# Identity products on the tensor engine in the waits of a kernel's first ten slots

## The chip, the cores and the metric

The kernel runs on one core of a Trainium2 chip. The metric is the device time of one execution in microseconds. A core has a tensor engine (PE, with its weight loads shown apart as PEld), a vector engine (DVE), a scalar engine (ACT), a general engine (POOL) and a queue engine for transfers (SP). Each takes its instructions in the order in which the program issues them, and waits for the results of others by semaphores. The profile also shows the clock that PE was granted, as a share of its full speed.

## What is computed

Top-k attention over 8 batches, 8 heads, 576 positions and 64 elements per head, and behind it an MLP with an exact GELU on 4608 tokens (512 to 2048 to 512). All is f32.

```python
scores = scale * np.matmul(q, k.transpose(0, 1, 3, 2))
kth = np.partition(scores, -32, axis=-1)[..., -32:-31]
scores = np.where(scores >= kth, scores, -1e9)
attn = softmax(scores)                      # over the last axis
x = (attn @ v).transpose(0, 2, 1, 3).reshape(4608, 512)
h = x @ w_in
out = (0.5 * h * (1 + erf(h / sqrt(2)))) @ w_out
```

## The kernel before

**Items and slots.** Heads are taken in pairs. An item is one tile of 128 query rows for the two heads of a pair (or the 64-row tails of two pairs together): 144 items. The main loop (line 651) runs over slots n, and each slot works on several items at different stages: scores of item n+2, softmax of item n-1, transposes of item n-2, attention of item n-3, top-k of item n. Order is written out by hand: the pool is scheduled manually, so each engine's instructions stand in the order of the code.

**A slot on PE**, in order: `scores` (a 128x128 product t_ps, line 283, and products s_ps, line 287); `attend` (o, line 466; only where an item completes a pair of row tiles: slots 4, 6, 8 and 10 among the first eleven; the variable `product` tells it); then `transposes` in three pieces, first the tail (tp_t, line 411), then one main piece of four transposes per head (tp, line 429); and, where due, pieces of `transpose_qk` for later pairs (tp_qk, line 242), which `prep` holds. In between `mlp(1)` issues pieces of the MLP (h_ps, line 518; y_ps, line 554), as far as finished tokens allow. The first 256 tokens are finished by the attention of slot 10 (START is 10), so in slots 0 to 9 these calls issue nothing.

**A slot on ACT**: copies of the scores out of PSUM (lines 297 and 298), softmax of the first head (lines 379 and 380), the copy of an attention product into xT (line 471), softmax of the second head, copies of the tail and the main transposes (lines 412 and 436), copies of q/k pieces (line 246), and up to slot 16 the conversion of a unit of weights (`weights_size`, lines 175 to 179).

**DVE** does the top-k: eight MAX8 (line 340) and six MATCH_REPLACE8 (line 343) per item, and at its end the reciprocal of the denominator of the item before (line 366). **POOL** adds the weight words (lines 194 and 206), adds a small number to the denominators (line 372), computes the threshold and the bias (lines 355 and 358) and multiplies the item before by the reciprocals (`normalise`, line 392); the tail transpose of that item needs this product.

**PSUM.** t_ps, o, tp_t, tp and tp_qk share two buffers of the tag tp, so each waits until the one before last has been copied away. s_ps has one buffer. h_ps has two of the tag l1, unused until slot 10 except by the warming products below.

**Before the loop** line 630 issues nine (WARM) products of a zero tile, then the q/k pieces of two pairs and the scores of items 0 and 1.

Of the kernel before, what the change touches and what calls it, by code (L numbers as in the profile page):

```python
# [14 lines left out]
def kernel(  # L15
# [19 lines left out]
    nc = tc.nc  # L35
    f32, i32, u32 = mybir.dt.float32, mybir.dt.int32, mybir.dt.uint32
# [5 lines left out]
    P = 128  # L42
# [19 lines left out]
    ps = ctx.enter_context(tc.tile_pool(name="ps", bufs=2, space=bass.MemoryType.PSUM))  # L62
    ctx.enter_context(tc.manual_schedule())

    ident = const.tile([P, P], f32, name="ident")
# [59 lines left out]
    START = 2 * NP + 2  # L125
    WARM = 9
# [54 lines left out]
    def on_pool(u):  # L181

        return u in words and SLOT_OF[u] >= START + 2
# [3 lines left out]
    def weights_add(u):  # L187
        if u in words:
            w, _, below, d = parts(u)
            if on_pool(u):  # L190
                nc.gpsimd.tensor_scalar(
                    w.bitcast(i32), w.bitcast(u32), 2.0**-13, None, op0=ALU.mult
                )
            nc.gpsimd.tensor_tensor(d, d, below, op=ALU.add)
            if not ends_late(u):
                weights_end(u)
        made.add(u)

    def ends_late(u):

        return u in words and SLOT_OF[u] <= START

    def weights_end(u):
        if u in words:
            w, _, _, d = parts(u)
            nc.gpsimd.tensor_tensor(d, d, w.bitcast(i32), op=ALU.add)
# [118 lines left out]
    def top_k(i, hooks):  # L325


        stat_of[i] = st = {
            "top": work.tile([P, 2, TOPK], f32, tag="top", name="top"),
            "neg": work.tile([P, 2, 2], f32, tag="neg", name="neg"),  # L330
            "bias": work.tile([P, 2], f32, tag="bias", name="bias"),
            "den": work.tile([P, 2], f32, tag="den", name="den"),
            "rden": work.tile([P, 2], f32, tag="rden", name="rden"),
        }
        cur = [row(i, e) for e in range(2)]
        rest = work.tile([P, 2, S], f32, tag="rest", bufs=1, name="rest")
        n_op = 0
        for r in range(TOPK // 8):
            for e in range(2):
                nc.vector.max(st["top"][:, e, 8 * r : 8 * r + 8], cur[e])  # L340
            if r < TOPK // 8 - 1:
                for e in range(2):
                    nc.vector.match_replace(  # L343
                        rest[:, e], st["top"][:, e, 8 * r : 8 * r + 8], cur[e], LOWEST
                    )
                cur = [rest[:, e] for e in range(2)]
            if r in hooks:
                hooks.pop(r)()

    def threshold(i):  # L350

        if i < 0 or i >= N:
            return
        st = stat_of[i]
        nc.gpsimd.tensor_scalar(  # L355
            st["neg"], st["top"][:, :, 0 :: TOPK - 1], -1.0, None, op0=ALU.mult
        )
        nc.gpsimd.tensor_tensor(
            st["bias"], st["neg"][:, :, 0], st["neg"][:, :, 1], op=ALU.subtract
        )  # L360

    def inverse(i):
        if i < 0 or i >= N:
            return
        st = stat_of[i]
        nc.vector.reciprocal(st["rden"], st["den"])  # L366

    def add_small(i):
        if i < 0 or i >= N:
            return  # L370
        st = stat_of[i]
        nc.gpsimd.tensor_scalar(st["den"], st["den"], 1e-9, None, op0=ALU.add)  # L372

    def softmax(i, e):

        if i < 0 or i >= N:
            return
        st, s = stat_of[i], row(i, e)
        nc.scalar.activation(s, s, func=AF.Prelu, bias=st["neg"][:, e, 1:2], scale=1.0, alpha=STEEP)  # L379
        nc.scalar.activation(  # L380
            s, s, func=AF.Exp, bias=st["bias"][:, e : e + 1], scale=1.0,
            accum_out=st["den"][:, e : e + 1],
        )
# [16 lines left out]
    def transposes(i):  # L400

        if i < 0 or i >= N:
            return []
        t, s = items[i][1], S_of.pop(i)

        def tails():
            tp = ps.tile([P, 512], f32, tag="tp", name="tp_t")
            if t < NM:
                if t % 2 == 0:
                    pt_now[0] = work.tile([P, 2 * NM + 1, 2 * P], f32, tag="pt", name="pt")  # L410
                nc.tensor.transpose(tp[:, 0:P], s[:, SM : S + TL], ident)  # L411
                nc.scalar.copy(out=pt_now[0][:, 2 * NM, t % 2 * P : (t % 2 + 1) * P], in_=tp[:, 0:P])  # L412
            else:
                pt_now[0] = ptt
                for r in range(2):
                    nc.tensor.transpose(
                        tp[0:TL, r * P : (r + 1) * P], s[:, r * S + SM : (r + 1) * S], ident
                    )
                for e in range(2):
                    c = slice(e * TL, (e + 1) * TL)  # L420
                    nc.scalar.copy(
                        out=halves(ptt[c, 0, NM, :], e, NJ * P), in_=halves(tp[0:TL, 0 : 2 * P], e, P)
                    )

        def main(e):
            tp = ps.tile([P, 512], f32, tag="tp", name="tp")
            first = e * (S + TL if t < NM else S)
            for j in range(NM):
                nc.tensor.transpose(  # L429
                    tp[:, j * P : (j + 1) * P], s[:, first + j * P : first + (j + 1) * P], ident  # L430
                )
            if t < NM:
                dst = pt_now[0][:, e * NM : (e + 1) * NM, t % 2 * P : (t % 2 + 1) * P]
            else:
                dst = ptt[:, e, 0:NM, :]
            nc.scalar.copy(out=dst, in_=tp.rearrange("p (j n) -> p j n", j=NM))  # L436

        return [tails] + [lambda e=e: main(e) for e in range(2)]

    def copy_x():  # L440
        while copies:
            copies.pop()()
# [149 lines left out]
    def run_gelus():  # L592
        while waiting:
            gelus(waiting.pop(0))
# [9 lines left out]
    def mlp(n):  # L604
        for _ in range(n):
            if done[0] >= len(pieces) or pieces[done[0]][0] > ready[0] or left[0] == 0:
                return
            pieces[done[0]][1]()
            done[0] += 1
            left[0] -= 1  # L610
            if eager[0]:
                run_gelus()
# [12 lines left out]


    idle = raws["v"][0][:, NM].rearrange("p e d -> p (e d)")
    warm = ps.tile([P, 512], f32, tag="l1", name="warm")
    for _ in range(WARM):
        nc.tensor.matmul(warm[:, 0:P], lhsT=idle, rhs=idle, start=True, stop=True)  # L630
    for pair in range(2):
        for piece in transpose_qk(pair, pair == 0):
            piece()
# [17 lines left out]
    for n in range(ahead):  # L651

        left[0] = 4 if n in (START, START + 1) else 8
        eager[0] = n > N
        weights_add(unit_in(n))
        scores(n + 2)
        product = attend(n - 3)
        late = n > START
        if n <= START:

            softmax(n - 1, 0)
        copy_x()
        mlp(1)
        tr = transposes(n - 2)
        if product and n > START and done[0] < len(pieces) and pieces[done[0]][0] > ready[0]:

            for piece in tr[:1]:
                piece()
            tr, ready[0] = tr[1:], n_tok[0]
        if n > START:  # L670
            softmax(n - 1, 0)
        mlp(1)
        if not late:
            softmax(n - 1, 1)
        mlp(1)
        prep = prep_in.pop(n, [])
        if len(prep) > 1 and len(tr) == 3:
            tr, prep = tr[:1] + prep[:1] + tr[1:], prep[1:]
        for piece in tr[:-1]:
            piece()  # L680
            ready[0] = n_tok[0]
            mlp(1)
        ready[0] = n_tok[0]
        if late:
            softmax(n - 1, 1)
        add_small(n - 1)
        if ends_late(unit_in(n)):
            weights_end(unit_in(n))
        for piece in tr[-1:] + prep:
            piece()  # L690
            mlp(1)

        run_gelus()
        mlp(left[0])
        run_gelus()
        if n < N:
            top_k(n, {3: lambda: inverse(n - 1)})
        else:
            inverse(n - 1)
        threshold(n)  # L700
        u = unit_in(n + 1)

        normalise(n - 1, 2 if on_pool(u) else 0)

        weights_size(unit_in(n + 1))
        if n >= FIRST:
            load_weights(n + 2)
        if n <= NP:
            load("v", n)
# [38 lines left out]
```

## Time and profile before

| quantity | value |
|---|---|
| median of 5 runs | 1642.16 us (1640.52 to 1642.37) |
| the profiled execution | 1640.55 us, span 1638.8 us |
| PE busy | 1587.8 us (97% of the span) |
| DVE busy | 1415.3 us (86%) |
| ACT busy | 1186.2 us (72%) |
| POOL busy | 662.3 us (40%) |
| mean granted PE clock | 0.979 |

The span is from the first to the last instruction on the engines. In the lines of the profile, L12 is line 12 of the kernel; out<-in are the program's names; a bracket shows how long the engine stood idle before the instruction and what ended that.

### The profile page before, as it was taken

The numbers are of one execution on the slowest core, as the hardware profiler recorded it, in microseconds if no ns is written. First come the engines' busy times: TensorE is split into PE (matmuls) and PEld (weight loads), VectorE is DVE, ScalarE is ACT, GpSimd is POOL, SyncE is SP. The second block draws the span as 40 slices with busy tenths as digits, with TensorE's granted clock in tenths as the row PEclk, the third lists the DMA queues.
The fourth block names the chain that finished last, engine by engine and source line by source line (L and its number), as shares of the span: only waits on it lengthen the run. The fifth ranks groups of instructions, "written<-read, shape, count | busy, mean of one in ns | idle before, by whom it ended". The sixth has DMA issues, their size and how long they took to land.

```text
span 1638.8 us, 25030 instructions
## 1 busy us (share of the span) xinstructions
PE 1587.8 (97%) x8818; PEld 1075.5 (66%) x8818; DVE 1415.3 (86%) x3046; ACT 1186.2 (72%) x2133; POOL 662.3 (40%) x759
## 2 busy tenths in 40 slices
PE   6679999999999999999999999999999999999999
PEld 4346676766666666676666667676666666666665
DVE  8999999988898889998989898998889889999800
ACT  6999877777777777777777777777777777777720
POOL 4897633333333333333333333333333333333300
PEclk7779999999999999999999999999999999999999
DMA  6433210011101120001100111001110101000000
GB/s 164 141 112 122 55 43 1 14 32 41 35 1 28 30 50 8 14 16 36 30 28 15 28 30 43 1 14 32 41 36 1 28 16 35 1 14 3 6 13 13
DMA packets 126765, 56.14 MB, mean 34 GB/s; under 512 B 117776, under 2 KB 118064, under 8 KB 126640
## 3 DMA queue, kind: packets, MB, share of 16 engines
q1 hardware_dynamic: 125376, 54.12, 12.3%
q8 instruction: 70, 1.15, 0.3%
q14 instruction: 55, 0.45, 0.1%
q10 hardware_dynamic: 1200, 0.39, 0.1%
q0 software_dynamic: 64, 0.03, 0.0%
HBM read 45.08 MB, written 9.44 MB: 33 GB/s over the span
## 4 chain that ended last, share of the span: by engine, by line
PE 91%; ACT 5%; POOL 1%; issue 1%; DVE 1%; DMA 1%; SPq 0%; ACTq 0%; POOLq 0%; DVEq 0%
PE y_ps L554 30%; PE h_ps L518 30%; PE o L466 9%; PE tp L429 8%; PE s_ps L287 8%; PE tp_qk L242 2%; PE t_ps L283 2%; PE o L477 1%; ACT s L380 1%; PE s_ps L314 1%; PE tp_t L411 1%; ACT s L379 1%; POOL s L392 1%; ACT w_in_sb L175 1%; ACT s L297 1%
## 5 line engine op out<-in xcount | busy, mean ns | idle before, releaser
L340 DVE MAX8 top<-rest 128x8 f32<-128x576 f32 x864 | 609.6, 747 | 0.0
L518 PE MATMUL h_ps<-xT,w_in_sb 128*128 128x256 f32 (+1 forms) x2560 | 553.0, 361 | 0.0
L554 PE MATMUL y_ps<-w_out_sb,g 128*128 128x512 f32 x1152 | 548.9, 599 | 0.0
L392 POOL TENSOR_SCALAR s<-s,rden 128x576 f32<-128x576 f32 x278 | 476.4, 1723 | 0.6 <-DVE rden L366 0.4
L518 PEld LDWEIGHTS h_ps<-xT,w_in_sb 128*128 128x128 f32 x2560 | 428.4, 191 | 61.8 <-issue 16.8
L343 DVE MATCH_REPLACE8 rest<-top,rest 128x576 f32<-128x576 f32 x576 | 423.5, 743 | 0.0
L372 POOL TENSOR_SCALAR den<-den 128x2 f32<-128x2 f32 x144 | 32.0, 222 | 836.7 <-ACT s L380 836.3
L554 PEld LDWEIGHTS y_ps<-w_out_sb,g 128*128 128x128 f32 x1152 | 195.1, 190 | 168.2 <-issue 167.3
L297 ACT ACTIVATE s<-s_ps 128x1024 f32<-128x1024 f32 x127 | 130.5, 1028 | 164.3 <-PE s_ps L287 142.1
L380 ACT ACTIVATE s<-s,bias 128x576 f32<-128x576 f32 x288 | 223.6, 776 | 13.2 <-ACT s L379 0.7
L379 ACT ACTIVATE s<-s,neg 128x576 f32<-128x576 f32 x288 | 224.5, 779 | 0.3 <-POOL neg L355 0.2
L436 ACT COPY pt<-tp 128x512 f32<-128x512 f32 x256 | 147.5, 576 | 101.5 <-PE tp L429 101.5
L429 PEld LDWEIGHTS tp<-ident,s 128*128 128x128 f32 x1152 | 145.6, 144 | 101.0 <-issue 58.9
L343 DVE MATCH_REPLACE8 rest<-top,s 128x576 f32<-128x576 f32 x288 | 211.8, 743 | 0.0
L340 DVE MAX8 top<-s 128x8 f32<-128x576 f32 x288 | 201.8, 742 | 1.4 <-ACT s L293 1.4
L429 PE MATMUL tp<-ident,s 128*128 128x128 f32 x1152 | 178.0, 278 | 14.2 <-ACT pt L412 11.6
L466 PE MATMUL o<-pt,raw_v 128*64 128x256 f32 x1280 | 155.7, 390 | 0.0
L287 PE MATMUL s_ps<-qk 64*128 64x256 f32 x1024 | 152.5, 418 | 0.8 <-ACT s L295 0.8
L366 DVE RECIPROCAL rden<-den 128x2 f32<-128x2 f32 x144 | 23.1, 161 | 138.3 <-POOL den L372 138.0
L466 PEld LDWEIGHTS o<-pt,raw_v 128*64 128x64 f32 x1280 | 87.8, 139 | 66.5 <-issue 22.6
L287 PEld LDWEIGHTS s_ps<-qk 64*128 64x128 f32 x1024 | 91.9, 194 | 23.7 <-issue 1.6
L529 ACT ACTIVATE g<-h_ps 128x512 f32<-128x512 f32 x144 | 78.6, 595 | 37.8 <-PE h_ps L518 37.1
(71 smaller groups left out, 1075.2 us busy)
## 6 DMA issues: line engine op xcount, KB each, us to landing
raw_q<-in_q_dram SPq DMA_DIRECT2D x64, 128.0 KB, 2.4
raw_v<-in_v_dram SPq DMA_DIRECT2D x64, 128.0 KB, 2.4
w_out_sb<-in_moe_w_in_dram SPq DMA_DIRECT2D x16, 511.8 KB, 4.9
raw_k<-in_k_dram SPq DMA_DIRECT2D x62, 128.0 KB, 2.4
out_dram<-y SPq DMA_DIRECT2D x31, 256.0 KB, 2.2
w_out_sb<-in_moe_w_out_dram SPq DMA_DIRECT2D x10, 511.8 KB, 3.9
words<-in_moe_w_out_dram SPq DMA_DIRECT2D x6, 511.8 KB, 4.5
out_dram<-y SPq DMA_DIRECT2D x9, 128.0 KB, 2.3
```

Of the source, the lines that this page charges most:

```text
L287: nc.tensor.matmul(s_ps[:, e, c * 256 : (c + 1) * 256], lhsT=lhsT[rows, :], rhs=qk[rows, KT + c * 256 : KT + (c + 1) * 256], start=True, s ...
L297: nc.scalar.activation(spread(s, S + TL, SM), s_ps, func=AF.Copy, scale=scale)
L340: nc.vector.max(st["top"][:, e, 8 * r : 8 * r + 8], cur[e])
L343: nc.vector.match_replace(rest[:, e], st["top"][:, e, 8 * r : 8 * r + 8], cur[e], LOWEST)
L379: nc.scalar.activation(s, s, func=AF.Prelu, bias=st["neg"][:, e, 1:2], scale=1.0, alpha=STEEP)
L380: nc.scalar.activation(s, s, func=AF.Exp, bias=st["bias"][:, e : e + 1], scale=1.0, accum_out=st["den"][:, e : e + 1],)
L392: (nc.vector if e >= 2 - on_dve else nc.gpsimd).tensor_scalar(s, s, st["rden"][:, e : e + 1], None, op0=ALU.mult)
L429: nc.tensor.transpose(tp[:, j * P : (j + 1) * P], s[:, first + j * P : first + (j + 1) * P], ident)
L436: nc.scalar.copy(out=dst, in_=tp.rearrange("p (j n) -> p j n", j=NM))
L466: nc.tensor.matmul(o[e * D : (e + 1) * D, 0:n], lhsT=vt[:, j, e, :], rhs=pt[:, e * NM + j if j < NM else 2 * NM, :], start=(j == 0), stop= ...
L518: nc.tensor.matmul(h_tile(u)[:, i, :], lhsT=w_in_sb[:, ko, f * P : (f + 1) * P], rhs=xT[:, ko, c0 : c0 + n], start=(ko == 0), stop=(ko == ...
L554: nc.tensor.matmul(y_of[sub], lhsT=g_of[u][:, i, sub * P : (sub + 1) * P], rhs=w_out_sb[:, f, :], start=(f == 0), stop=(f == FT - 1),)
```

## The change

A helper `keep_busy` issues a number of products of one matrix with itself into a PSUM tile that nobody reads; the warming products before the loop now go through it. In slots 0 to 9 the loop calls it with the identity: 8 products in slot 0 and in slots with an attention product, 28 in the others, ahead of the transposes; 10 more behind the tail transpose in slots with an attention product; and 24 at the end of slot 1's pieces.

```diff
     idle = raws["v"][0][:, NM].rearrange("p e d -> p (e d)")
-    warm = ps.tile([P, 512], f32, tag="l1", name="warm")
-    for _ in range(WARM):
-        nc.tensor.matmul(warm[:, 0:P], lhsT=idle, rhs=idle, start=True, stop=True)
+
+    def keep_busy(count, m):
+        warm = ps.tile([P, 512], f32, tag="l1", name="warm")
+        for _ in range(count):
+            nc.tensor.matmul(warm[:, 0:P], lhsT=m, rhs=m, start=True, stop=True)
+
+    keep_busy(WARM, idle)
...
         mlp(1)
+        if n < START:
+
+            keep_busy(8 if product or n == 0 else 28, ident)
         prep = prep_in.pop(n, [])
...
         for piece in tr[:-1]:
             piece()
+            if n < START and product and piece is tr[0]:
+                keep_busy(10, ident)
             ready[0] = n_tok[0]
             mlp(1)
...
         for piece in tr[-1:] + prep:
             piece()
             mlp(1)
+        if n == 1:
+            keep_busy(24, ident)
```

## The prediction

> **What bounds the kernel now.** First the page's slices (41 us each; digits are tenths busy): they part the run into two regimes.
>
> ```profile
> PE   6679999999999999999999999999999999999999
> DVE  8999999988898889998989898998889889999800
> ACT  6999877777777777777777777777777777777720
> PEclk7779999999999999999999999999999999999999
> ```
>
> From the fourth slice on PE is full at the full clock; only the first three slices (the ten slots that the change touches) have PE slack and a granted clock near 0.7. So no gain or loss arises late, but any shift of the moment at which PE fills up is carried to the end one for one.
>
> Next the busy time in the stretches between the steps of the clock (columns: stretch, length, busy time and count of each engine, granted clock, DMA share, GB/s).
>
> ```profile
> 17.64:55.10 37.46, 22.66 (x88) 14.90 (x90) 37.46 (x81) 32.62 (x52) 27.68 (x24) 0.50 0.50 128
> 55.10:65.30 10.20, 4.40 (x33) 2.62 (x29) 10.02 (x23) 9.62 (x17) 8.04 (x8) 1.00 0.71 231
> 65.30:72.10 6.80, 5.41 (x23) 3.78 (x25) 6.80 (x15) 6.02 (x11) 6.44 (x6) 0.51 0.31 71
> 72.10:79.00 6.90, 4.20 (x33) 2.51 (x31) 6.90 (x16) 6.52 (x13) 5.84 (x5) 0.99 0.37 137
> 79.00:92.60 13.60, 8.50 (x37) 5.38 (x37) 13.60 (x31) 12.69 (x19) 13.00 (x12) 0.50 0.37 120
> 103.00:113.20 10.20, 7.66 (x31) 5.00 (x33) 10.20 (x23) 9.32 (x18) 9.33 (x9) 0.50 0.29 86
> ```
>
> The clock is either whole or half, and stretches are multiples of about 3.4 us. DVE is full throughout: a slot of top-k is 9.7 us on DVE whatever PE does. ACT is nearly as full. A warm PE can therefore win only where ACT or PE, not DVE, decides.
>
> Third the order of time on ACT and PE around slots 2 and 3.
>
> ```profile
> 29.20 0.80 PE L283 MATMUL t_ps<-qk 128*128 128x128 f32 x2 [2.82 <-ACT qk L246]
> 29.93 2.08 PE L287 MATMUL s_ps<-qk 64*128 64x256 f32 x8
> 35.16 0.48 PE L411 MATMUL tp_t<-ident,s 128*128 128x128 f32 x1 [3.16 <-DMA w_out_sb<-in_moe_w_in_dram]
> ```
> ```profile
> 32.49 1.00 ACT L297 ACTIVATE s<-s_ps 128x1024 f32<-128x1024 f32 x1
> 36.75 0.25 ACT L412 COPY pt<-tp_t 128x128 f32<-128x128 f32 x1
> 48.97 0.59 ACT L436 COPY pt<-tp 128x512 f32<-128x512 f32 x1 [0.72 <-PE tp L429]
> ```
>
> Scores 4 leave PE at 32.01, and ACT, working without a break, takes them at 32.49: 0.5 us in hand. The DMA named on the third line had long landed; POOL's normalisation of item 0 ended at 35.1, and that is what PE waited for. ACT's only waits in the slots are the bracketed ones on PE's transposes: 0.72 us at half clock, 0.26 us in warm slots.
>
> Last, in the chain of waits, the price of 128-column f32 passes in a long row.
>
> ```profile
> 291.21 2.68 PE h_ps L518 x24
> 293.89 0.22 PE t_ps L283 x2
> ```
>
> **The change part by part.** The sum is made against the profiled execution, 1640.55 us (span 1638.8 and 1.75 around it). The median, 1642.16, is 1.6 above it; the runs lie in two clusters, 1640.5 and 1642.2.
>
> *Price of a product.* An f32 product of 128 columns is two passes. 24 passes in 2.68 us are 0.112 each, so 0.223 a product at the full clock (t_ps: 0.22). The far ends: the nine products of line 630 stood 3.67 us, 0.41 each; a transpose (one pass) steps on in 0.11. I take 0.223, the row with the same shape and the longest run. Blocks: 8 are 1.8 us, 10 are 2.2, 24 are 5.4, 28 are 6.25. In all 8+52+28+28+3x18+3x28 = 254 products, 57 us, beside PE's 43.7 us of idle time in the first 110 us (110 less 66.3 busy); they fit only if old work runs warm.
>
> *Slot 0.* Eight products run from 16.5 to 18.3, inside the 2.42 us wait for raw_k (next start 18.97): hidden. The clock, which fell at 17.64 in the trace, should hold; then tp_qk takes 0.65 instead of 1.09, and ACT, which waits for it, starts its conversion 0.44 earlier.
>
> *Slot 1.* PE: tp_qk 0.44, t_ps 0.22, s_ps 1.06 from 18.97 reach 20.7. 28 products end at 26.95; the two q/k pieces (0.22 and 0.44) at 27.6, their ACT copies due at 27.9 (28.31 less 0.44): still hidden. Then 24 more to 33.0. Behind them in PE's order stand scores 4: 0.22 + 1.14 to 34.3. ACT is ready at 32.05 and now waits 2.3 us; everything behind on ACT (softmax 1, copies, weight conversions) stands with it. L297 comes at 34.4 instead of 32.49: **+1.9**.
>
> *Slot 2.* 28 products from 34.25 to 40.5, but POOL is done near 35, so these delay the tail transpose of item 0 from 35.16 to 40.5, done 40.75. ACT would be there at 38.65: 2.1 us more, **+4.05** in all. Warm transposes give 0.45 back: **+3.6**.
>
> *Slots 3 to 9.* Without an attention product PE needs, from ACT's tail copy on: main transposes 0.44, scores 0.22 + 1.06, 28 products 6.25, tail 0.11, first main 0.66: 8.75 us; with one: 0.44 + 1.28 + 2.31 + 1.8 + 0.11 + 2.2 + 0.66 = 8.8. A slot is 9.7, so both stay about 0.9 us inside it and cost nothing; that cover goes if the clock halves, and then 28 products are about 12 us. Gain: the 0.72 us waits of slots 3, 5, 7 and 9 become 0.26: 4 x 0.46, to **+1.75**. POOL's add to the denominator waits for ACT, so DVE's reciprocal, which stood with 0.18 us to spare in slot 4, makes DVE wait about 3 us in slots 3 and 4. That is covered: DVE later idles 1.53, 1.00, 1.00 and 2.00 us (128, 140, 163, 185) and gives them up first. No DMA is moved; the loads are issued by the same steps, and SP's queue has nothing new. The new tiles use the l1 buffers, idle until slot 10.
>
> *Slot 10.* It has an attention product and no filler. Attention ends near 114.0; the tail needs POOL's item 8 (113.1 plus 2.4: 115.5), the first MLP product ACT's xT copy (114.66 plus 1.75 plus 0.36: 116.8). PE stands idle for nearly 3 us, just where before it was dense at half clock and then warm. The nearest row is the fall at 17.64, 1.1 us into an idle stretch and after a thin one; so I take a fall, and of the shortest stretch, 3.4 us, half is lost on work that the chain passes through (114.8 to 118.8 are MLP products and transposes on the chain): **+1.7**. Ends: 0, and 3.4 for two stretches.
>
> [...]
>
> *Sum.* 1.75 + 1.7 = 3.45 above 1640.55: **1644.0 us**. From 138 on PE is without a gap until 182, and again from 204, so the shift stays.
>
> **The rivals.**
>
> *Faster: the blocks are hidden in slots 1 and 2.* Place: PE ahead of scores 4 and of tail 0. It turns on the price of one product: ACT loses nothing if 80 products, 2.2 us of other work (0.66 q/k, 1.28 scores, 0.27 tail) from 20.7 on end by 36.3, a price of about 0.167 us. For it: transposes step in 0.11, and these products use one stationary operand over and over. Against: 24 passes of the same shape cost 0.112 each. Then only the gains stay: 0.44 + 5 x 0.46 = 2.7, 1637.9 us, and up to 3.3 with the warm scores of slot 10: 1637.2. Chance 0.24.
>
> *Clearly slower: the clock falls early or twice.* If it is half from 17.6 to 24.5 as in the trace, the first block costs up to 2.8 us more: 1646.8; two stretches at slot 10 instead give 1645.7, a stretch lost in slots 3 to 9 about 1.2 more. For it: a window with 55% PE busy (1.88 of 3.4 us, 75.7 to 79.1) was followed by half clock. Against: filled slots have PE over 85% busy. Chance 0.31.
>
> *The products don't keep the clock, or cost 0.41 throughout.* 28 products are then about 12 us, beyond the slot: several us in each of seven slots, some 45 us in all, 1690. Against: after line 630's products the transposes at 5.28 ran four in 0.63, the warm duration. Chance 0.03.
>
> The forecast keeps 0.42, its own range 1642.3 to 1645.4.
>
> **How the numbers follow.** A measurement of this kernel tells 0.2% (3.3 us) from nothing: 1638.9 to 1645.4 is "within". The forecast lies within it whole (0.42); of the faster rival 0.20 lies below 1638.9 and 0.04 within; of the clearly slower one 0.29 lies above and 0.02 within; the last is above. So faster 0.20, within 0.48, slower 0.32. The range reaches from the faster rival's 1637.5 to 1648, an early fall together with one at slot 10; about 0.2 is left out.
>
> **What would show it.** Clock 1.00 from 14.6 to 113; products at 0.22; ACT's L297 at 34.4 with a wait on s_ps of 2.3, its L412 near 40.8 with a wait on the tail of 2.1; the 0.72 us waits gone; a DVE wait on the denominator in slots 3 or 4; a cold stretch after 114. Wrong if ACT runs through slots 1 and 2 without waiting, if a product's price isn't 0.22, or if the clock steps elsewhere.

## The result, and the profile after

The changed kernel takes 1643.86 us (median of 30 executions, 1643.57 to 1645.57); the kernel before, run beside it, 1640.89 us (median of 50, 1639.76 to 1642.57). The ratio is 1.0020, with a 95% interval of 1.0015 to 1.0025: slower by some 3 us. The interval leaves out 1, so a loss is there, but the time lies inside what the prediction called "within" (1638.9 to 1645.4). Before's times spread from 1639.8 to 1642.6, with 14 of the 50 under 1640.2 and 13 over 1642.0; of the five runs behind the 1642.16 shown earlier, three lay over 1642.0. The profiled execution of after took 1643.92 us, against 1640.55 us of the one before: +3.37 us.

The page's slices of after, 41 us each, first:

```profile
PE   8999999999999999999999999999999999999999
DVE  7999999988898989998989888998889888999800
ACT  5999877777777777777777777777777777777620
PEclk9999999999999999999999999999999999999999
```

The change did what it says: PE is full and its granted clock whole from the first slices on, where before they showed 6, 6, 7 and a clock of 7. The busy time by stretch confirms it (columns as before: stretch, length, busy time and count of PE, PEld, DVE, ACT and POOL, granted clock, DMA share, GB/s):

```profile
17.64:55.10 37.46, 36.27 (x303) 33.14 (x304) 35.05 (x77) 30.20 (x48) 23.73 (x22) 1.00 0.45 118
55.10:113.20 58.10, 56.63 (x466) 47.72 (x462) 57.30 (x124) 55.42 (x91) 52.55 (x41) 1.00 0.40 128
113.20:130.00 16.80, 14.25 (x90) 10.74 (x88) 16.80 (x38) 15.57 (x26) 15.70 (x12) 1.00 0.45 128
```

In the first stretch PE went from 22.66 us busy at half clock to 36.27 at the whole one. Yet ACT did less in the same 37.46 us, 30.20 instead of 32.62, POOL too (23.73 for 27.68), and DVE was no longer full (35.05). The work came later, on a faster PE. The order of time says where; PE first (L632 is the line of the products; x56 are 28 of them, two passes each):

```profile
20.86 6.52 PE L632 MATMUL warm<-ident 128*128 128x128 f32 x56
27.87 5.52 PE L632 MATMUL warm<-ident 128*128 128x128 f32 x48
33.23 0.39 PE L283 MATMUL t_ps<-qk 128*128 128x128 f32 x2
33.55 1.14 PE L287 MATMUL s_ps<-qk 64*128 64x256 f32 x8
34.61 6.52 PE L632 MATMUL warm<-ident 128*128 128x128 f32 x56
40.97 0.27 PE L411 MATMUL tp_t<-ident,s 128*128 128x128 f32 x1
```

From 20.86 to 40.97 PE works without a pause, and most of it is products that nobody reads. The scores of item 4 stand behind 52 of them, the tail transpose of item 0 behind 28 more. ACT pays (the bracket is its idle time and what ended it):

```profile
34.73 1.02 ACT L297 ACTIVATE s<-s_ps 128x1024 f32<-128x1024 f32 x1 [2.39 <-PE s_ps L287]
41.27 0.27 ACT L412 COPY pt<-tp_t 128x128 f32<-128x128 f32 x1 [2.16 <-PE tp_t L411]
43.79 1.27 ACT L175 ACTIVATE w_in_sb<-w_out_sb,low 128x1024 int32<-128x1024 int16 x1
```

Before, neither copy waited, and they started at 32.49 and 36.75. DVE, which was full before, now waits too:

```profile
52.01 0.17 DVE L366 RECIPROCAL rden<-den 128x2 f32<-128x2 f32 x1 [2.41 <-POOL den L372]
62.61 0.17 DVE L366 RECIPROCAL rden<-den 128x2 f32<-128x2 f32 x1 [0.80 <-POOL den L372]
```

The chain of waits between 17 and 45 us (start, length, what) is made of these products:

```profile
20.93 6.45 PE warm L632 x56
...
28.03 5.36 PE warm L632 x48
...
33.62 1.06 PE s_ps L287 x8
34.68 6.45 PE warm L632 x56
41.13 0.11 PE tp_t L411
```

A conversion of weights on ACT (line 175) starts once a slot and is a good clock hand for the shift. The start of that conversion, from the orders of time of several kernels:

| kernel | slot 1 | 2 | 3 | 4 | 5 | 6 | 7 | 8 | 9 | 10 | 11 |
|---|---|---|---|---|---|---|---|---|---|---|---|
| before | 20.57 | 29.04 | 39.83 | 50.30 | 59.95 | 69.57 | 79.05 | 88.67 | 98.61 | 108.52 | 119.27 |
| after | 20.16 | 28.71 | 43.79 | 54.08 | 63.85 | 73.17 | 82.70 | 91.93 | 102.27 | 111.78 | 122.63 |
| after less before | -0.41 | -0.33 | +3.96 | +3.78 | +3.90 | +3.60 | +3.65 | +3.26 | +3.66 | +3.26 | +3.36 |
| without the 24 (e1_no24) | 20.02 | 28.56 | 39.38 | 49.67 | 60.35 | 69.57 | 79.13 | 88.36 | 98.71 | 108.20 | 119.04 |
| e6_best | 20.04 | 28.58 | 38.74 | 48.89 | 58.66 | 67.98 | 77.56 | 86.80 | 97.31 | 106.81 | 117.67 |

The whole loss arises between slots 2 and 3; slots 3 to 10 give 0.60 us of it back; +3.36 at slot 11 is what the end shows too (+3.37).

### The profile page after: what moved, and what is told of

It is laid out like the page before. It is cut to its first block, busy times and chain, and to the rows that moved or that the text cites. A ratio compares the mean times of both kernels' runs of the same rounds, so it can differ in the third digit from the quotient of the medians.

```text
span 1642.2 us, 26046 instructions
## 1 busy us (share of the span) xinstructions
PE 1625.9 (99%) x9326; PEld 1121.5 (68%) x9326; DVE 1415.4 (86%) x3046; ACT 1187.8 (72%) x2133; POOL 662.6 (40%) x759
## 4 chain that ended last, share of the span: by engine, by line
PE 93%; ACT 3%; POOL 1%; DVE 1%; issue 1%; SPq 0%; DMA 0%; ACTq 0%; DVEq 0%; POOLq 0%
PE y_ps L554 30%; PE h_ps L518 30%; PE o L466 8%; PE s_ps L287 8%; PE tp L429 7%; PE warm L632 2%; PE tp_qk L242 2%; PE t_ps L283 2%; PE o L477 1%; PE tp_t L411 1%; PE s_ps L314 1%; ACT s L380 1%; POOL s L392 1%; ACT s L379 1%; ACT w_out_sb L179 0%
## 5 line engine op out<-in xcount | busy, mean ns | idle before, releaser
L297 ACT ACTIVATE s<-s_ps 128x1024 f32<-128x1024 f32 x127 | 130.6, 1028 | 166.7 <-PE s_ps L287 144.5
L429 PE MATMUL tp<-ident,s 128*128 128x128 f32 x1152 | 173.0, 273 | 2.4 <-ACT pt L412 1.8
L466 PE MATMUL o<-pt,raw_v 128*64 128x256 f32 x1280 | 152.3, 384 | 0.0
L287 PE MATMUL s_ps<-qk 64*128 64x256 f32 x1024 | 145.2, 402 | 0.8 <-ACT s L295 0.8
L529 ACT ACTIVATE g<-h_ps 128x512 f32<-128x512 f32 x144 | 78.6, 595 | 37.8 <-PE h_ps L518 37.1
L287 PEld LDWEIGHTS s_ps<-qk 64*128 64x128 f32 x1024 | 88.1, 186 | 22.0 <-ACT s L295 1.0
```

What stands on the lines that cost most here:

```text
L287: nc.tensor.matmul(s_ps[:, e, c * 256 : (c + 1) * 256], lhsT=lhsT[rows, :], rhs=qk[rows, KT + c * 256 : KT + (c + 1) * 256], start=True, s ...
L297: nc.scalar.activation(spread(s, S + TL, SM), s_ps, func=AF.Copy, scale=scale)
L429: nc.tensor.transpose(tp[:, j * P : (j + 1) * P], s[:, first + j * P : first + (j + 1) * P], ident)
L466: nc.tensor.matmul(o[e * D : (e + 1) * D, 0:n], lhsT=vt[:, j, e, :], rhs=pt[:, e * NM + j if j < NM else 2 * NM, :], start=(j == 0), stop= ...
```

## The experiments

The theory: the products are worth little as warmers, because DVE and ACT, not PE, set a slot; they cost where the program's order on PE puts them ahead of something that ACT waits for, and that is in slots 1 and 2. The rivals: the time was lost in slots 3 to 9 (conversions slowed, the denominators late); it was lost to the clock at slot 10; or the products' own kind matters. Where a kernel has fewer or other products, only work that nobody reads is left out. Times stand beside the kernel before, run on the same chip, whose median was 1640.9 beside e1 to e4 and 1641.2 beside the others.

**The block of 24, alone taken away.**

```diff
-        if n == 1:
-            keep_busy(24, ident)
```

> The block of 24 products at the end of slot 1 is left out; the rest is as in the changed kernel. Theory (scores 4 stand behind the block on PE, and ACT stands behind scores 4): the wait of 2.39 us on ACT at L297 goes, and the wait of 2.16 us at L412 in slot 2 shrinks to about 0.4, since the 28 products of slot 2 then run from 30.1 to 36.4 and ACT wants the tail at 36.3. That is 4.2 to 4.4 us back: about 1639.5, 1.4 us below the kernel before. Rival A (the cost is spread: the products lengthen ACT's instructions and waits in every filled slot): only the 2.4 us come back, about 1641.5. Rival B (the block is needed to keep the clock): half clock after 31, a block of 28 takes 12 us somewhere, over 1645.

Measured: 1640.6 us, ratio 0.9999 (0.9990 to 1.0008): all of the loss is gone with 24 of 254 products. ACT's order of time:

```profile
32.03 1.03 ACT L297 ACTIVATE s<-s_ps 128x1024 f32<-128x1024 f32 x1
36.86 0.27 ACT L412 COPY pt<-tp_t 128x128 f32<-128x128 f32 x1 [0.45 <-PE tp_t L411]
60.35 1.25 ACT L175 ACTIVATE w_out_sb<-w_out_sb,low 128x1024 int32<-128x1024 int16 x1 [0.79 <-DMA w_out_sb<-in_moe_w_out_dram]
```

The wait before L297 is gone, the one before L412 fell from 2.16 to 0.45 us, and slot 3 begins 4.41 us earlier than in after (39.38 for 43.79). At slot 6 only 3.60 of that is left: the third line shows why. ACT, now early, waits 0.79 us for a transfer of weights that SP issued at 54.80. The 3.60 and this wait together are the 4.4 us, and the wait is about the 0.8 us by which the profiled run (1640.32) lies over the expected 1639.5.

**Fewer products where one wait was left.** Besides the 24, slot 2 has 20 instead of 28.

```diff
-            keep_busy(8 if product or n == 0 else 28, ident)
+            keep_busy(8 if product or n == 0 else 20 if n == 2 else 28, ident)
...
-        if n == 1:
-            keep_busy(24, ident)
```

> The block of 24 is left out and slot 2 has 20 products in place of 28, which end at 34.6, before POOL has normalised item 0. Theory: both waits of ACT in slots 1 and 2 are gone, 0.4 us less than without the 24 alone: about 1639.0, 1.9 us below the kernel before; ACT reaches L175 of slot 3 about 0.9 us earlier than before (39.83). Rival A (spread cost): no lower than 1641.5. Rival C (DVE's slots decide the first 120 us, so a warm clock gains nothing): 1640.9, the time before.

Measured: 1641.62 us, 1639.25 to 1643.17, ratio 1.0003 (0.9994 to 1.0012). Slot 3 starts at 38.65, 0.73 us ahead of e1, where 0.4 was expected; but ACT waits for the weights again (0.58 us), and the times fall apart by their mean granted clock: 1639.3 to 1639.5 in the two runs at 1.000, 1639.8 and 1640.1 at 0.999, 1641.6 to 1643.2 in the seven at 0.998 and under. The profiled one has a fall, right behind slot 11. Busy time by stretch:

```profile
123.47:126.88 3.41, 1.41 (x11) 0.86 (x9) 3.14 (x7) 3.38 (x9) 3.24 (x3) 1.00 0.84 258
126.88:130.29 3.41, 3.34 (x14) 2.10 (x16) 3.07 (x7) 3.38 (x6) 2.93 (x4) 0.50 0.89 362
```

A stretch of 3.41 us in which PE was busy for 1.41 is followed by 3.41 us at half clock. The longest pause in it was this one, 1.39 us, the idle time before t_ps:

```profile
126.95 0.80 PE L283 MATMUL t_ps<-qk 128*128 128x128 f32 x2 [1.39 <-ACT pt L436]
```

So the gain from slot 2 is real, and the runs at the whole clock come near the expected 1639.0. That new falls at the first slots behind the products take it away in most runs is read off the mean clocks; only the profiled run shows where its fall lies.

**Products in slots 0 to 2 alone.**

```diff
-        if n < START:
+        if n < 3:
...
-            if n < START and product and piece is tr[0]:
+            if n < 3 and product and piece is tr[0]:
```

> Products only in slots 0, 1 and 2 (8, 28 and 24, 28); none in slots 3 to 9. Theory: ACT is 4.0 us late at L175 of slot 3 as in the changed kernel, and the later slots, cold again as in the kernel before, give nothing back: 1640.9 + 4.0 = 1644.9, about 1 us above the changed kernel. Rival A (the cost lies in every filled slot): faster than the changed kernel, 1642 to 1643. ACT's conversions (L175 to L179) in slots 3 to 9 should show whether the 0.02 to 0.04 us that they are longer in the changed kernel come from the products.

Measured: 1647.08 us (1646.03 to 1648.05), ratio 1.0039 (1.0026 to 1.0051), 2.2 us more than expected. In the profiled run (1648.05 us) a part of that has nothing to do with the edit: the clock fell already in slot 0 (granted 0.80 from 14.20 to 17.55 and 0.70 from there to 21.00), where e3 and after have the same products (the 16 passes there took 3.04 us instead of 2.05) and slot 3 began at 45.16, 1.37 us later than in after. From there to slot 11 it took 80.98 us; after took 78.84 and before 79.44. Two groups of lines on ACT over these eight slots, e3 first (columns: busy us, mean ns of one | idle time before), then after:

```profile
L177 ACT ACTIVATE w_out_sb<-w_out_sb,high 128x1024 int32<-128x1024 int16 x8 | 9.9, 1236 | 0.3
L436 ACT COPY pt<-tp 128x512 f32<-128x512 f32 x16 | 9.4, 585 | 4.3 <-PE tp L429 4.3
```
```profile
L177 ACT ACTIVATE w_out_sb<-w_out_sb,high 128x1024 int32<-128x1024 int16 x8 | 10.3, 1283 | 0.3
L436 ACT COPY pt<-tp 128x512 f32<-128x512 f32 x16 | 9.2, 587 | 1.9 <-PE tp L429 1.6
```

Without the products ACT waits 2.7 us longer for main transposes (4.3 for 1.6), and its conversions are shorter, 1236 ns as before. So the products of slots 3 to 9 are worth 80.98 - 78.84 = 2.1 us against no products (0.97 of it a wait for weights that e3 has and after has not), and 0.6 us against the kernel before. That rival falls: slots 3 to 9 are a gain, though a small one.

**The block of 24 doubled.**

```diff
-            keep_busy(24, ident)
+            keep_busy(48, ident)
```

> The block at the end of slot 1 is doubled, from 24 to 48 products. Theory: the block is on the chain product by product, so 24 more at 0.227 us cost 5.4 us: 1643.9 + 5.4 = 1649.3, ACT's wait at L297 grows from 2.4 to 7.8 us, and DVE's wait for the denominator in slot 3 from 2.4 to about 8. Rival D (there is slack on DVE, which idles 5.5 us later, that takes up the delay): well under 1649, about 1646.

Measured: 1651.41 us (1649.6 to 1651.89), ratio 1.0065 (1.0051 to 1.0079). ACT's order of time:

```profile
39.85 1.02 ACT L297 ACTIVATE s<-s_ps 128x1024 f32<-128x1024 f32 x1 [7.75 <-PE s_ps L287]
46.40 0.27 ACT L412 COPY pt<-tp_t 128x128 f32<-128x128 f32 x1 [2.17 <-PE tp_t L411]
```

The wait grew from 2.39 to 7.75 us: by 5.36, which is 24 times 0.223. The lowest run, which is the profiled one, is 5.8 us over after's usual 1643.8; 0.54 of that is a wait for weights in slot 5. The median is 7.5 us over after's; the three slowest runs have mean clocks of 0.998 and 0.999, and what they lost was not traced. With no slack of ACT left, each of the 24 products cost its own length, 0.223 us, and nothing downstream gave it back.

**Products into slots 10 and 11.** Six ahead of the tail transpose of slot 10, six at the end of slot 11, in another PSUM tile.

```diff
+        if n == START:
+            keep_busy(6, ident, "l2")
...
+        if n == START + 1:
+            keep_busy(6, ident, "l2")
```

> The changed kernel with 6 products more in slot 10, ahead of the tail transpose (a wait of 1.34 us), and 6 at the end of slot 11 (a wait of 1.39 us). Theory (a third of the changed kernel's runs, 1645.2 us at a mean clock of 0.999, lose the clock for one stretch of 3.4 us in the thin slots 10 and 11): the upper group goes, all runs lie at 1643.8 with a clock of 1.000. Rival E (the clock falls somewhere in slots 0 to 9): two groups as before. Rival F (any product in slots 10 and 11 delays the MLP's products behind it): 1 to 2 us above 1643.8.

Measured: 1643.94 us (1643.74 to 1644.74), ratio 1.0016 (1.0007 to 1.0025). Nine of 11 runs lie at 1643.7 to 1644.2 with a mean clock of 1.000, two at 1644.7 with 0.999. After has 20 of 30 at 1643.6 to 1644.0 and ten at 1644.9 to 1645.6, again with 0.998 or 0.999. So filling the slots behind the products doesn't lower the usual time: that time holds no loss to the clock. That it thins out the upper group is possible, but two of 11 and ten of 30 don't tell it.

**The products as transposes.** Each identity product becomes two transposes of the identity (in this kernel the products' line is 636).

```diff
-            nc.tensor.matmul(warm[:, 0:P], lhsT=m, rhs=m, start=True, stop=True)
+            if m is idle:
+                nc.tensor.matmul(warm[:, 0:P], lhsT=m, rhs=m, start=True, stop=True)
+            else:
+                for h in range(2):
+                    nc.tensor.transpose(warm[:, h * P : (h + 1) * P], m, ident)
```

> The changed kernel with each product of the identity (two passes) replaced by two transposes of it (one pass each, the same 0.22 us); the nine products before the loop stay. If the clock follows how full PE is, whatever it does: 1643.9 and a clock of 1.000. If transposes do not count as work for the clock, as the long cold stretch from 17.6 to 55.1 in the kernel before suggests (38.1 to 41.5 was 97% busy, half of it transposes, and stayed cold): the clock falls near 17 and blocks of 28 take 12.5 us at half clock, more than a slot: some 45 us more in all, about 1690.

Measured: 1643.53 us (1642.96 to 1645.76), ratio 1.0018 (1.0009 to 1.0028). PE's order of time and two stretches of it:

```profile
20.62 6.33 PE L636 MATMUL warm<-ident 128*128 128x128 f32 x56
27.44 5.40 PE L636 MATMUL warm<-ident 128*128 128x128 f32 x48
```
```profile
100.00:110.00 10.00, 9.74 (x82) 8.66 (x81) 10.00 (x22) 9.44 (x16) 8.90 (x8) 1.00 0.28 105
130.00:140.00 10.00, 9.35 (x51) 6.69 (x52) 9.05 (x21) 9.85 (x16) 8.46 (x7) 0.83 0.30 122
```

Two transposes cost nearly what one product does (28 pairs took 26.79 - 20.62 = 6.17 us, 28 products 6.35), and they hold the clock through slot 9 as well (1.00 from 100 to 110). The fall comes behind them, after 130 (0.83 from 130 to 140). For the clock the kind of filler made no difference here (the run's mean clock is 0.999).

**Products from slot 3 on only.** None in slots 0 to 2, the block of 24 gone with them.

```diff
-        if n < START:
+        if 3 <= n < START:
...
-        if n == 1:
-            keep_busy(24, ident)
```

> Products only from slot 3 on (no block in slots 0, 1 and 2, nor the 24). Theory: slots 1 and 2 run as in the kernel before, without ACT's waits, but slot 3's block of 28 starts at half clock near 42.5; with two stretches of 3.4 us until the clock rises it ends near 52.5 in place of 49, and ACT, due at the tail at 47.5, waits 5 us: 1640.9 + 5 - 0.6 = 1645. Rival A (the cost lies in every filled slot, not in slots 1 and 2): 1643 to 1644, with no wait of ACT over 1 us in slot 3. Rival H (the cold start costs nothing): 1640.

Measured: 1642.79 us (1640.87 to 1646.31), ratio 1.0014 (1.0005 to 1.0023), with mean clocks of 0.989 to 0.994. Slot 3's block starts at half clock (granted 0.50 from 30.00 to 43.30, 1.00 from there to 50.00):

```profile
42.57 6.84 PE L632 MATMUL warm<-ident 128*128 128x128 f32 x56
```
```profile
49.56 0.27 ACT L412 COPY pt<-tp_t 128x128 f32<-128x128 f32 x1 [1.78 <-PE tp_t L411]
```

In the profiled run it rose 0.7 us into the block, so 28 products took 6.84 us and ACT waited 1.78 us, not the 5 expected of a block that runs cold for longer. The runs over 1645.9 have the lowest clocks (0.989). This block came out the longer for starting at half clock (after's 28 in slot 2 took 6.52 us), just when it was not yet of use.

**The version put together.** No block of 24, 22 products in slot 2, six each in slots 10 and 11, and in slot 3 SP issues the next unit of weights ahead of the q and k loads (line numbers of the helper and below are shifted by nine).

```diff
+    put_off, slot = [], [-1]
+    def loads_now():
+        while put_off:
+            x = put_off.pop(0)
+            load("q", x)
+            load("k", x)
...
-                load("q", pair + 2)
-                load("k", pair + 2)
+                put_off.append(pair + 2)
+                if slot[0] != 3:
+                    loads_now()
...
-            keep_busy(8 if product or n == 0 else 28, ident)
+            keep_busy(8 if product or n == 0 else 22 if n == 2 else 28, ident)
+        if n == START:
+            keep_busy(6, ident, "l2")
...
-        if n == 1:
-            keep_busy(24, ident)
+        if n == START + 1:
+            keep_busy(6, ident, "l2")
...
             load_weights(n + 2)
+        loads_now()
```

> No block of 24, 22 products in slot 2 in place of 28, the products in slots 10 and 11 as in the run before, and in slot 3 the weight load is issued ahead of the q and k loads in SP's queue. Theory: ACT waits in slots 1 and 2 gone (-4.4 from 1643.8), clock held in every run, and the wait of 0.6 to 0.8 us for the weights at slot 5 gone: 1638.8, 2.1 us below the kernel before (1640.9), with a spread under 1 us. Rival C (a warm clock gains nothing, DVE decides): 1640 or more. Rival G (with ACT earlier, POOL's normalisation or another load becomes the next wait): 1639.5.

Measured: 1639.02 us (1638.71 to 1643.08), against 1641.23 beside it, ratio 0.9991 (0.9982 to 0.9999): 0.3% under after, and under before by 2.2 us of medians, which is less than the 0.2% that one measurement tells; the interval only just leaves out 1. Six of 11 runs lie at 1638.7 to 1639.0, below the lowest of 33 runs of before (1639.88). SP's order of time, e6 first, then before, shows the weights 5 us earlier:

```profile
49.43 0.82 SPq L160 DMA_DIRECT2D w_out_sb<-in_moe_w_out_dram  x2
```
```profile
54.43 0.98 SPq L160 DMA_DIRECT2D w_out_sb<-in_moe_w_out_dram  x2
```

ACT takes them without a wait at 58.66, 1.29 us ahead of before. The run at 1643.08 has a mean clock of 0.995: falls still come now and then, and the expected spread of under 1 us was missed. The move of the loads was not tried by itself.

## Why the prediction was right, step by step

The sum was 1644.0 us; the profiled run gave 1643.92, the median 1643.86. The case that came true is the forecast: the blocks of slots 1 and 2 delay ACT. But two terms of the sum were off, in opposite directions.

- *The price of a product* (0.223 us). 28 of them with the start of the next piece took 27.21 - 20.86 = 6.35 us, 0.227 each; 24 took 33.23 - 27.87 = 5.36, 0.223 each. Right. It refutes the faster rival, whose blocks fit below 0.167, and the one with 0.41.
- *Slot 0* (hidden, 0.44 earlier). The clock held, and ACT's first conversion started at 20.16 instead of 20.57: 0.41 earlier. Right.
- *Slot 1* (a wait of 2.3, L297 at 34.4, +1.9). Wait 2.39, L297 at 34.73, +2.24. Right in kind, 0.33 low: the first block started 0.16 later (20.86 for 20.7) and took 0.1 more, and the scores behind the 24 took 0.1 more.
- *Slot 2* (a wait of 2.1, L412 at 40.8, +4.05, then 0.45 back to +3.6). Wait 2.16, L412 at 41.27, +4.52, slot 3 at +3.96: right in kind, 0.36 low, of which 0.33 came from slot 1. e1 and e4 show that the two waits are nearly all that the block of 24 does: without it the waits shrink by 2.39 and 1.71 us and slot 3 starts 4.41 us earlier, and 24 more add 5.36 to the first wait.
- *Slots 3 to 9* (four waits of 0.72 become 0.26; 1.84 back, to +1.75). This term failed in size: 0.60 came back. The waits did shrink as predicted; ACT's waits for PE over these slots, before first, then after (total us, times, longest):

```profile
ACT pt L436 <- PE tp L429: 3.9, 8, 0.7
ACT qk L246 <- PE tp_qk L242: 1.0, 2, 0.7
```
```profile
ACT pt L436 <- PE tp L429: 1.6, 6, 0.5
ACT qk L246 <- PE tp_qk L242: 1.1, 3, 0.7
ACT pt L412 <- PE tp_t L411: 0.2, 1, 0.2
```

  That is 4.9 to 2.9 us, 2.0 less. But ACT's busy time over the same eight slots rose from 73.22 to 74.39 us. Of these 1.17 us, 0.7 are the weight conversions (line 177 from 1235 to 1283 ns, line 179 from 1132 to 1159, eight of each, line 175 by some 13 ns, nine). With the products gone in e3 line 177 is back at 1236, so that stretching comes with them; 79.44 - 2.0 + 1.17 is 78.6, and 78.84 was measured. Where the other 0.45 of ACT's busy time lies I couldn't assign to one group. I had priced the conversions at nothing, because nothing in the change touches ACT.
- *DVE's waits for denominators* (about 3 us in slots 3 and 4, covered later). 2.41 and 0.80 us, 3.2 in all. The shift at the end (+3.37) is the one of slot 11 (+3.36), so these waits left no trace of their own. That DVE gives the 3.2 us back from its later idle time was not tried by itself.
- *Slot 10* (the clock falls for one stretch, +1.7; ends 0 and 3.4). This term failed: in the profiled run, and in 20 of 30, the clock held, and the cost was 0. I had PE idle for nearly 3 us there:

```profile
113.16 2.38 PE L466 MATMUL o<-pt,raw_v 128*64 128x256 f32 x20
116.87 0.33 PE L411 MATMUL tp_t<-ident,s 128*128 128x128 f32 x1 [1.34 <-POOL s L392]
117.04 1.03 PE L518 MATMUL h_ps<-xT,w_in_sb 128*128 128x256 f32 x4
118.42 0.66 PE L429 MATMUL tp<-ident,s 128*128 128x128 f32 x4 [0.35 <-ACT xT L471]
```

  The pause is 1.34 us, and then come short ones: the MLP product started at 117.04, ahead of slot 10's xT copy (ACT, 118.01), and not behind it, as I had it. By the code the first MLP piece reads only the first two of the four pairs, which were copied in earlier slots. In ten of 30 runs the mean clock is 0.998 or 0.999 and the time 1.4 us higher: that fits a fall of the size that I priced. Their traces weren't taken, so neither the fall nor its place is shown.
- *The sum.* +3.96 at slot 3 instead of +3.6, 0.60 back instead of 1.84, 0 instead of 1.7 at slot 10: +3.36 against +3.45. So the total is nearer than its terms deserve; the first three steps carried the sign, and that the errors of the last two cancelled was luck.
- *What goes with a fall.* I had read two marks off the row at 17.64, an idle stretch and a thin one ahead of it. The length of the pause doesn't part the runs: after's 1.34 us at slot 10 had no fall, and in e2 the longest pause was 1.39 us and the clock fell. How full the stretches ahead of before's and e2's steps were is in the last section.
- *The other rivals.* A fall of the clock in slot 0, priced for the clearly slower case, was seen in e3's profiled run (0.70 granted from 17.55 to 21.00, slot 3 at +5.33 instead of +3.96); none of after's 30 times reached that case's 1646.8, the highest being 1645.57. The 1690 case is out by the price of a product and by the clock of 1.00 from 17 to 113.

## What to carry to other kernels

PE ran its instructions in the program's order here (24 products more, in e4, put ACT's copy of the scores behind them 5.36 us further back). Filler placed so costs nothing only up to the slack of the first thing behind it that another engine waits for; work that slack out in the trace, in the filler's own unit (here 2.39 us of wait in slot 1 are some eleven products too many, 2.16 us in slot 2 some ten), before choosing a count. What a warmer engine can give is bounded by the waits on it along the engine that sets the pace: 4.9 us of ACT's waits in eight slots here, of which 2.0 went and 0.6 arrived. And a version that makes the leading engine earlier meets the next resource that was just in time, here a transfer of weights.

## What the runs showed of the hardware that was not expected

**In before the clock's steps lie 3.41 us or a multiple of it apart.** They stand at 17.64, 55.19, 65.43, 72.26, 79.08, 92.74, 102.98 and 113.22 us, with 0.50 and 1.00 granted in turn; the stretches between them are 37.55, 10.24, 6.83, 6.82, 13.66, 10.24 and 10.24 us, which is 11, 3, 2, 2, 4, 3 and 3 times 3.41. In e2 a fall at 126.88 and a rise at 130.29 are 3.41 us apart. Three of before's stretches of that length (columns as before): the first was 60% busy, and the clock stayed whole; the second was 55% busy, and the clock fell behind it; the third was 95% busy, and the clock stayed half.

```profile
58.60:62.02 3.42, 2.04 (x14) 1.41 (x14) 3.24 (x9) 3.13 (x5) 3.20 (x5) 1.00 0.41 92
75.67:79.08 3.41, 1.86 (x12) 1.43 (x14) 3.41 (x8) 3.12 (x10) 2.35 (x3) 1.00 0.00 0
38.12:41.54 3.42, 3.26 (x15) 2.24 (x15) 3.42 (x9) 3.04 (x5) 3.34 (x4) 0.50 0.08 16
```

Cut into 3.41 us from 7.41 to 113.21, before has 31 such stretches. Ahead of its four falls PE was busy for 48, 4, 55 and 8% of the stretch; in the seven after which the whole clock stayed, for 60 to 78%. Ahead of its four rises PE was busy throughout; in the 16 after which the clock stayed half, for 21 to 95%. In e2 it was 41% ahead of the fall and 98% ahead of the rise. That is one trace and two steps of another: whether the busy share is what decides, and from which share on, was not tried, and the busy times of matmuls are modelled. After's trace shows no step from 17 to 1640 us, though PE was busy for just 51% of the 3.41 us from 115.00 and 41% of those from 128.20; with no step near them, it isn't shown where its stretches begin.

**Executions of one program form groups.** After's times lie at 1643.8 and 1645.2, e2's spread over 3.9 us, each with its mean granted clock (e2: 1.000 at 1639.4, 0.997 at 1643.0). One stretch at half clock takes 3.41 x 0.5 / 1640 = 0.001 off the mean, so by estimate after's upper group has one fall and e2's slowest runs three. Counted back in steps of 3.41 us, the steps begin at another distance from the start of the span from trace to trace (0.6 us in before and e2, 2.3 in e8, 2.6 in e3); that this is the cause of the groups was not tried.

**Conversions on ACT took 4% longer beside the products.** Line 177 (int16 to int32, 128x1024) took 1235 ns before, 1283 in after, 1236 in e3 over the same slots. f32 copies out of PSUM didn't change (line 436: 587 ns in both). The whole clock alone didn't do it: before's two in the stretches at the whole clock from 55.19 and from 92.74 took 1225 and 1237 ns. Why was not looked into.

**An issue on SP took 1 us longer than its neighbours.** In e1 one q/k load took 1.58 us to issue:

```profile
51.34 1.58 SPq L92 DMA_DIRECT2D raw_k<-in_k_dram  x1
```

Before, the same kind took 0.59. The weights behind it were issued at 54.80, and ACT waited 0.79 us for them. Before, ACT began 5.52 us after that issue and after 5.64, e1 5.55 with a wait: this transfer was just in time all along, and any gain ahead of it needs it moved, as e6 does. The long issue isn't needed for the wait: in e3 and e4 none was long, ACT came 6.58 and 6.30 us after the issue and still waited 0.97 and 0.54 us.
